# New durations for VectorE and ScalarE in the table that an order of instructions is planned with

## The chip, the cores and the metric

The kernel runs on one core of a Trainium2 chip. The metric is the device time of one execution in microseconds; three runs of the kernel before gave 955.95 to 956.46 us, with a median of 956.35 us. The engines are TensorE (PE in the profile, its weight loads PEld), VectorE (DVE), ScalarE (ACT), GpSimd (POOL) and SyncE (SP), which here issues DMAs. Every engine works through its own instructions strictly in the order in which the program lists them, and an instruction that waits for another engine holds up all that stand behind it on its own.

## The reference

Three layers follow each other, all in float32:

```python
# 1. attention, 8 batches x 8 heads, 576 positions of 64, causal by blocks of 64 positions
scores = q @ k.T / sqrt(64);  scores = where(block_i >= block_j, scores, -1e9)
attn = exp(scores - max); attn /= attn.sum() + 1e-9; x = attn @ v        # then 4608 tokens x 512
# 2. a feed-forward layer, 512 -> 2048 -> 512
h = x @ w_in
g = where(h > 0, h, exp(min(h, 0)) - 1);  y = g @ w_out
# 3. a soft mixture of 8 experts with 4 slots each
logits = y @ phi                                                          # 4608 x 32
d = softmax over tokens;  c = softmax over slots
slot_out = relu((d.T @ y) @ w1[e]) @ w2[e];  out = c @ slot_out
```

## The kernel before

The work has a prologue, a long middle part and a tail. In the prologue the weights are brought in and split: each word of `w_in` is rescaled, shifted and put together by bit operations (L424 or L426, L428, L431), and split into a high and a low float32r part (L441, L442). Beside it the first pairs of heads go through the attention. In the middle part 36 tiles of 128 tokens go through the second layer, 22 units of planning time apart, while TensorE works ahead on the attention of later pairs of heads. The tail computes the experts and writes the result.

One tile has four ranges of 512 columns of the second layer. A range is 12 matmuls in 4 blocks of three (`hm`, L808 to L810: high times high, high times low, low times high), with weights from `w0` to `w3`, one for each range. ScalarE then takes the exponential (L813), VectorE takes the minimum and subtracts 1 (L815), then takes the maximum with the matmul's result in PSUM (L818), and transposes (L826). Two PSUM banks take turns: range `r` uses bank `r % 2`, so the first matmul of a range waits until L818 of the range two before it has read the bank. A tile's routing follows: logits (L853), a copy (L876), sums (L880, L881), maxima (L885 to L894), two exponentials, a transpose on TensorE (L360 with `base` alone, "the turn"), a copy of its result (L904), and the weighted sum of slots (L919 on TensorE, L924 on VectorE).

The attention of a pair of heads has four groups of score matmuls (L568 to L576), each followed by fills with the mask (L584), row maxima (L587), exponentials (L590), sums and reciprocals (L602, L603), a scaling on GpSimd (L607), transposes by TensorE (L360 with `base` and `att`) or VectorE (L689) and the product with the values (L739 or L767).

None of this order is written out. Each operation is added to a plan with its engine or engines, a duration, what it reads and writes, and a priority (`key`). `Plan.order` (L126) is a list scheduler: it keeps a clock for each engine, starts an operation when the engine is free by the table's duration and its inputs have come by the table's durations plus a delay for each pair of engines (`HOPS`, L60: 0.13 to 0.23), and takes the ready one with the lowest key. Where an operation may run on two engines (copies on ScalarE or VectorE by `CP2`, the rescaling on ScalarE or GpSimd), the one that is free first takes it. Where TensorE would stand idle in two stretches of the program, the planner puts in small matmuls that compute nothing needed (L1200, `plan.fill`). The sequence that comes out is issued as it is; on the chip the engines wait for each other's semaphores, not for the planner's clock.

So a duration in the table costs no time itself. It moves instructions on all engines, picks the engine of some copies and sets the number of small matmuls.

Of the kernel before, what the change touches and what calls it, by code (L numbers as in the profile page):

```python
# [14 lines left out]
AF = mybir.ActivationFunctionType  # L15
# [3 lines left out]
P = 128  # L19
# [219 lines left out]
def attention_moe_kernel(ctx: ExitStack, tc, q, k, v, w_in, w_out, phi, w1, w2, consts, out):  # L239
# [103 lines left out]
    def cpdur(n, big=False):  # L343
        return (0.05 + n / 1200, 0.065 + n / 960)

# [203 lines left out]
    def wide(x):  # L549
        return S if x == "b" else P * (x[0] + 1)  # L550

    def pair_scores(n, fill, key):
# [32 lines left out]
        for x in units:  # L585
            c = nm_col + 9 * s + UNITS[x][0]
            add("DVE", 0.08 + wide(x) / 960, lambda e, x=x, c=c: nc.vector.tensor_reduce(  # L587
                out=f(c, 1), in_=pb(at(x), wide(x)), axis=AX.X, op=ALU.max, negate=True),
                r=keys(x), w=[("nm", s, x)], key=key)
            add("ACT", 0.50 + wide(x) / 1300, lambda e, x=x, c=c: nc.scalar.activation(  # L590
                f(pat(x, n), wide(x)), pb(at(x), wide(x)), AF.Exp, bias=f(c, 1), scale=1.0,
                accum_out=f(sum_col + 9 * s + UNITS[x][0], 1)),
                r=keys(x) + [("nm", s, x)], w=[pkey(x, n), ("sum", s, fill // 2)], key=key)

    def pair_weights(n, half, key):
# [8 lines left out]
        add("DVE", 0.35, rec, r=[("sum", s, half)], w=[("rs", s, half)], key=key)  # L604
        for x in units:
# [71 lines left out]
    def pair_swap(n, half, key):  # L677
# [5 lines left out]
        for x in HALVES[half]:  # L683
            if x == "b" or x[0] == 0:
                continue
            cs = min(x[0] + 1, 3)
            at, _, step = spots(x[0], x[1], 0)
            o = f(px, 4 * XW).rearrange("p (m b j) -> p b m j", m=4, j=32)[:, at:at + step * (cs - 1) + 1:step]
            add("DVE", 0.12 + P * cs / 960, lambda e, x=x, o=o, cs=cs: nc.vector.transpose(  # L689
                out=o, in_=f(pat(x, n), P * cs).rearrange("p (c m i) -> p c m i", c=cs, m=4)),  # L690
                r=[pkey(x, n)], w=[("px", sl, x)], key=key)
        both = f(py, 2 * YW).rearrange("p (h w) -> p h w", h=2)
        groups = ([("b", c) for c in range(4)], [((3, 0), 3), ((3, 1), 3), ("b", 4)]) if half == 0 else ([((0, 0), 0), ((0, 1), 0)],)
        for gi, blocks in enumerate(groups):
# [8 lines left out]
            def evac(e, g=g, tb=tb):  # L703
# [7 lines left out]
                else:  # L711
                    copy(e, both[:, :, 0:P], pb(tb, 256).rearrange("p (h x) -> p h x", h=2))
            add(*evict(n, (560, 430, 256)[g]), evac, r=[tk], w=[("py", sl, g)], key=key)
        if half == 0:
# [71 lines left out]
    def tile_split(i, key):  # L786
        s = i % 2
        r0 = (P * i) % RING
        halves = sorted({(P * i // S) % 2, ((P * i + P - 1) // S) % 2})
        xr_keys = [("xr", p, hf, j) for p in range(4) for hf in halves for j in range(2)]  # L790
        xv = f(XR, 4 * RING).rearrange("p (c t) -> p c t", t=RING)[:, :, r0:r0 + P]
        xh, xl = XH + 512 * s, XL + 512 * s
        add("ACT", 0.52, lambda e: nc.scalar.copy(fr(xh, 512).rearrange("p (c t) -> p c t", t=P), xv),  # L793
            r=xr_keys, w=[("xh", s)], key=key)
        add("POOL", 1.35, lambda e: nc.gpsimd.tensor_tensor(  # L795
            out=fr(xl, 512).rearrange("p (c t) -> p c t", t=P), in0=xv,
            in1=f(xh, 512).rearrange("p (c t) -> p c t", t=P), op=ALU.subtract),
            r=xr_keys + [("xh", s)], w=[("xl", s)], key=key)

    def tile_range(i, r, hb, gs, ts, kr):  # L800
# [4 lines left out]
        for kk in range(4):  # L805
# [62 lines left out]
    def tile_dispatch(tiles, gs, banks, lps, dtx, dx, kp, later=False):  # L868
# [6 lines left out]
        for t in range(n):  # L875
            add("DVE", 0.2, lambda e, t=t: nc.vector.tensor_copy(f(lps[t][0], P), pb(banks[t][0], P)),  # L876
                r=[banks[t][1]], w=[lps[t][1]], key=kp)
# [6 lines left out]
        ko, kn = "nmx%d" % ((i + 1) % 2), "nmx%d" % (i % 2)  # L884
        add("DVE", 0.07 + n * P / 960, lambda e: nc.vector.tensor_reduce(out=f(MXT, 1), in_=pb(reps, n * P), axis=AX.X, op=ALU.max, negate=True),  # L885
            r=[bk], w=["mxt"], key=kp)
        add("DVE", 0.1, lambda e: nc.vector.tensor_tensor(out=f(nmn, 1), in0=f(nmo, 1), in1=f(MXT, 1), op=ALU.min),
            r=[ko, "mxt"], w=[kn], key=kp)
        add("ACT", 0.3 + n * 0.1, lambda e: nc.scalar.activation(f(dtx[0], n * P), pb(reps, n * P), AF.Exp, bias=f(nmn, 1), accum_out=f(TSUM, 1)),
            r=[bk, kn], w=[dtx[1], "tsum"], key=kp)  # L890
        add("ACT", 0.22, lambda e: nc.scalar.activation(f(ALPHA, 1), f(nmo, 1), AF.Exp, bias=f(nmn, 1), scale=-1.0),
            r=[ko, kn], w=["alpha"], key=kp + 0.1)
        for t in range(n):
            add("DVE", 0.1, lambda e, t=t: nc.vector.tensor_reduce(out=f(NMC + t, 1), in_=pb(tok + NS * t, NS), axis=AX.X, op=ALU.max, negate=True),  # L894
                r=[bk], w=[("nmc", t)], key=kp + 0.2)
            add("ACT", 0.4, lambda e, t=t: nc.scalar.activation(f(C + NS * (i + t), NS), pb(tok + NS * t, NS), AF.Exp, bias=f(NMC + t, 1),
                                                                accum_out=f(CS + i + t, 1)),
                r=[bk, ("nmc", t)], w=["c", "cs"], key=kp + 0.2)
# [5 lines left out]
        add("DVE", 0.1, lambda e: nc.vector.tensor_copy(f(dx[0], n * NS).rearrange("p (t s) -> p t s", t=n),  # L904
                                                        pb(flip, n * P).rearrange("p (t x) -> p t x", t=n)[:, :, 0:NS]),
            r=[fk], w=[dx[1]], key=kp)
        add("DVE", 0.1, lambda e: nc.vector.scalar_tensor_tensor(
            out=f(SSUM, 1), in0=f(SSUM, 1), scalar=f(ALPHA, 1), in1=f(TSUM, 1), op0=ALU.mult, op1=ALU.add),
# [326 lines left out]
```

## Time and profile before

| | us |
|---|---|
| median of 3 runs | 956.35 |
| the profiled execution | 955.77 |
| its span from the first to the last instruction | 954.0 |
| TensorE busy | 908.7 (95%) |
| VectorE busy | 675.9 (71%) |
| ScalarE busy | 439.4 (46%) |
| GpSimd busy | 272.6 (29%) |

"Busy" is the time in which at least one instruction of the engine is under way; instructions of one engine overlap at their ends, so the sum of their durations is larger. A matmul's record also runs on past the start of the next one. Idle time is put down to what the next instruction waited for.

### The profile page before, as it was taken

The page shows a single profiled execution, that of the slowest core. Times are in us where ns is not written, and L with a number is a line of the kernel's source. Part 1 is how long each engine was busy: PE and PEld are TensorE (multiplying, and loading weights), DVE is VectorE, ACT ScalarE, POOL GpSimd, SP SyncE. Part 2 cuts the span into 40 slices and gives each one's busy share as a digit, 9 for nine tenths or more (in the row PEclk, how much of TensorE's full clock was granted, in tenths as well). Part 3 has the DMA queues.
Part 4 walks back from the last instruction along what each step waited for, and adds up shares of the span by engine and source line. Part 5 has one row for each costly group of instructions (what it writes and reads, how often), then busy time and mean ns, then how long its engine had stood idle before and what let it go on. Part 6 is the DMA issues. An engine that isn't in the chain of part 4 may idle for free.

```text
span 954.0 us, 19403 instructions
## 1 busy us (share of the span) xinstructions
PE 908.7 (95%) x6708; PEld 623.3 (65%) x6708; DVE 675.9 (71%) x1718; ACT 439.4 (46%) x1285; POOL 272.6 (29%) x428
## 2 busy tenths in 40 slices
PE   8889999999999999999999999999999999999992
PEld 6556777666666766676766666766776776766350
DVE  5887795668787887777888878887887844333160
ACT  5775655445445535444445445444444333322143
POOL 2863442133342332222323432332332210000000
PEclk9999999999999999999999999999999999999996
DMA  9846755647777785767677777667756498068969
GB/s 235 243 130 171 220 184 159 146 115 207 202 203 218 197 209 184 212 181 211 194 203 206 199 208 201 202 188 203 206 163 217 144 305 340 3 216 298 377 223 342
DMA packets 253217, 197.08 MB, mean 207 GB/s; under 512 B 183232, under 2 KB 206400, under 8 KB 250048
## 3 DMA queue, kind: packets, MB, share of 16 engines
q1 hardware_dynamic: 251920, 195.55, 69.1%
q8 instruction: 54, 0.88, 0.4%
q10 hardware_dynamic: 1200, 0.30, 0.1%
q14 instruction: 43, 0.35, 0.1%
HBM read 125.52 MB, written 70.25 MB: 205 GB/s over the span
## 4 chain that ended last, share of the span: by engine, by line
PE 74%; DVE 8%; DMA 7%; SPq 4%; ACT 2%; issue 2%; POOL 1%; ACTq 0%; DVEq 0%; POOLq 0%
PE ps L808 13%; PE ps L810 11%; PE ps L809 11%; PE ps L360 8%; PE ps L576 7%; PE ps L739 7%; SPq L355 4%; PE ps L919 3%; PE ps L568 2%; PE ps L853 2%; DMA att<-swapped 2%; DMA swapped<-att 2%; PE ps L767 2%; DVE base L587 2%; PE ps L460 1%
## 5 line engine op out<-in xcount | busy, mean ns | idle before, releaser
L808 PE MATMUL ps<-w,xhl 128*128 128x512 f32 x576 | 249.8, 434 | 7.8 <-DVE g L818 5.5
L607 POOL TENSOR_SCALAR att<-att,base 128x128 f32<-128x128 f32 (+4 forms) x288 | 181.0, 647 | 222.2 <-DVE base L603 151.0
L810 PE MATMUL ps<-w,xhl 128*128 128x512 f32 x576 | 226.8, 394 | 0.0
L809 PE MATMUL ps<-w,xhl 128*128 128x512 f32 x576 | 225.7, 392 | 0.0
L590 ACT ACTIVATE att<-ps,base 128x128 f32<-128x128 f32 (+4 forms) x288 | 157.4, 552 | 122.9 <-DVE base L587 121.0
L587 DVE TENSOR_REDUCE base<-ps 128x1 f32<-128x128 f32 (+4 forms) x288 | 135.7, 503 | 21.3 <-PE ps L572 12.2
L808 PEld LDWEIGHTS ps<-w,xhl 128*128 128x128 f32 x576 | 108.8, 189 | 52.0 <-issue 19.1
L813 ACT ACTIVATE xe<-ps 128x512 f32<-128x512 f32 x144 | 86.0, 600 | 115.0 <-PE ps L810 113.7
L810 PEld LDWEIGHTS ps<-w,xhl 128*128 128x128 f32 x576 | 108.1, 188 | 24.9
L336 ACT COPY att<-ps 128x128 f32<-128x128 f32 (+3 forms) x192 | 75.7, 434 | 95.8 <-PE ps L360 90.6
L809 PEld LDWEIGHTS ps<-w,xhl 128*128 128x128 f32 x576 | 108.9, 189 | 14.8
L815 DVE TENSOR_SCALAR xe<-xe 128x512 f32<-128x512 f32 x144 | 68.1, 473 | 67.0 <-ACT xe L813 65.6
L576 PE MATMUL ps<-att 64*128 64x128 f32 (+3 forms) x512 | 96.1, 468 | 1.0 <-ACT att L590 1.0
L360 PE MATMUL ps<-base,att 128*128 128x128 f32 (+1 forms) x496 | 83.2, 282 | 9.7 <-POOL att L607 8.5
L360 PEld LDWEIGHTS ps<-base,att 128*128 128x128 f32 (+1 forms) x496 | 58.0, 143 | 44.5 <-POOL att L607 17.6
L795 POOL TENSOR_TENSOR xhl<-xe,xhl 128x512 fp32r<-128x512 f32 x36 | 46.3, 1291 | 133.1 <-ACT xhl L793 127.0
L818 DVE TENSOR_TENSOR g<-xe,ps 128x512 f32<-128x512 f32 x108 | 73.3, 680 | 2.4
L689 DVE STREAM_TRANSPOSE att<-att 128x384 f32<-128x384 f32 x144 | 70.4, 507 | 5.3 <-POOL att L607 4.2
L739 PE MATMUL ps<-att 128*64 128x64 f32 (+4 forms) x864 | 71.9, 318 | 1.2 <-DMA att<-swapped 0.7
L576 PEld LDWEIGHTS ps<-att 64*128 64x128 f32 x512 | 42.0, 185 | 40.6 <-issue 14.1
L739 PEld LDWEIGHTS ps<-att 128*64 128x64 f32 x864 | 46.8, 137 | 32.3 <-issue 23.6
L826 DVE STREAM_TRANSPOSE g<-g 128x512 f32<-128x512 f32 x84 | 58.0, 695 | 1.7 <-DMA turned<-g 0.2
(134 smaller groups left out, 1115.1 us busy)
## 6 DMA issues: line engine op xcount, KB each, us to landing
turned<-g SPq DMA_DIRECT2D x60, 512.0 KB, 3.1
swapped<-att SPq DMA_DIRECT2D x24, 1024.0 KB, 4.6
g<-turned SPq DMA_DIRECT2D x120, 96.0 KB, 2.6
att<-in_moe_w_dram SPq DMA_DIRECT2D x11, 1024.0 KB, 11.8
att<-swapped SPq DMA_DIRECT2D x48, 192.0 KB, 3.9
att<-in_v_dram SPq DMA_DIRECT2D x64, 128.0 KB, 3.2
g<-in_moe_w_in_dram SPq DMA_DIRECT2D x16, 512.0 KB, 5.3
w_late<-in_moe_w_dram SPq DMA_DIRECT2D x8, 1024.0 KB, 6.9
```

What stands on the lines that cost most here:

```text
L336: nc.scalar.copy(o, i)
L360: mm(o, lhsT=i, rhs=f(IDN + base, n, base, base + n), start=True, stop=True, is_transpose=True)
L576: mm(pb(at((u, h)), P * (u + 1)), lhsT=f(qt + P * u, P, 64 * h, 64 * h + 64), rhs=f(kt, P * (u + 1), 64 * h, 64 * h + 64), start=True, sto ...
L587: add("DVE", 0.08 + wide(x) / 960, lambda e, x=x, c=c: nc.vector.tensor_reduce(out=f(c, 1), in_=pb(at(x), wide(x)), axis=AX.X, op=ALU.max, ...
L590: add("ACT", 0.50 + wide(x) / 1300, lambda e, x=x, c=c: nc.scalar.activation(f(pat(x, n), wide(x)), pb(at(x), wide(x)), AF.Exp, bias=f(c, ...
L607: add("POOL", (0.28 + wide(x) / 1050) * (1.3 if n < 8 else 1.0), lambda e, x=x, p=p: nc.gpsimd.tensor_scalar(out=f(p, wide(x)), in0=f(p, w ...
L739: mm(pb(o, w, 64 * h, 64 * h + 64), lhsT=f(vs + 320 * h + D * c, D), rhs=rhs(h), start=start, stop=stop)
L808: mm(pb(bank, 512), lhsT=fr(xh + P * kk, P), rhs=hi, start=(kk == 0), stop=False)
L809: mm(pb(bank, 512), lhsT=fr(xh + P * kk, P), rhs=lo, start=False, stop=False)
L810: mm(pb(bank, 512), lhsT=fr(xl + P * kk, P), rhs=hi, start=False, stop=(kk == 3))
L813: add("ACT", 0.48, lambda e: nc.scalar.activation(f(ee, 512), pb(bank, 512), AF.Exp), r=[("h", hb)], w=[("e", hb)], key=kr)
L818: add("DVE", 0.6, lambda e: nc.vector.tensor_tensor(out=f(g, 512), in0=f(ee, 512), in1=pb(bank, 512), op=ALU.max), r=[("e", hb), ("h", hb) ...
```

## The change

Nineteen lines of the kernel's plan get other durations for VectorE and ScalarE; no operation, buffer, priority or dependency is touched. The core of it:

```diff
     def cpdur(n, big=False):
-        return (0.05 + n / 1200, 0.065 + n / 960)
+        return (0.165 + n / 1200, 0.15 + n / 960)
...
-            add("DVE", 0.08 + wide(x) / 960, lambda e, x=x, c=c: nc.vector.tensor_reduce(
+            add("DVE", 0.14 + wide(x) / 960, lambda e, x=x, c=c: nc.vector.tensor_reduce(
...
-        add("ACT", 0.48, lambda e: nc.scalar.activation(f(ee, 512), pb(bank, 512), AF.Exp),
+        add("ACT", 0.6, lambda e: nc.scalar.activation(f(ee, 512), pb(bank, 512), AF.Exp),
...
-        add("DVE", 0.335, lambda e: nc.vector.tensor_scalar(
+        add("DVE", 0.47, lambda e: nc.vector.tensor_scalar(
...
-        add("DVE", 0.6, lambda e: nc.vector.tensor_tensor(
+        add("DVE", 0.68, lambda e: nc.vector.tensor_tensor(
```

`cpdur` gives a copy's duration on ScalarE and on VectorE. The others shown are L587, L813, L815 and L818. The rest is of the same kind: L602 with L603 (0.35 to 0.38), L689 (0.12 to 0.15 plus a part by size), the copies behind the transposes (L713), L793 (0.52 to 0.62), and the small operations of the routing (0.1 to 0.4 become 0.17 to 0.57). The durations for TensorE, GpSimd and the DMAs and the delays in `HOPS` stay.

In numbers of instructions: TensorE has 504 small matmuls (L1200) instead of 456. VectorE has 70 copies from PSUM (L338) instead of 56 and ScalarE has 12 instructions fewer. Two rescalings move from GpSimd to ScalarE. The 576 blocks of three matmuls stand in 247 uninterrupted runs instead of 236.

The order is changed nearly everywhere. Three places follow. The first is on VectorE where range 3 of tile 3 ends (its L818 frees the bank for range 1 of tile 4). Before, with `base` the area of the routing's small results, `xe` the exponentials and `g` the layer's result:

```order
L907 SCALAR_TENSOR_TENSOR base<-base 128x1
L904 COPY base<-ps 128x32
L924 SCALAR_TENSOR_TENSOR base<-base,ps 128x512
L815 TENSOR_SCALAR xe<-xe 128x512
L584 MEMSET ps 64x64 x2
L818 TENSOR_TENSOR g<-xe,ps 128x512
```

The same L815 and L818 after the change:

```order
L815 TENSOR_SCALAR xe<-xe 128x512
L876 COPY base<-ps 128x128
L587 TENSOR_REDUCE base<-ps 128x1 x4
L818 TENSOR_TENSOR g<-xe,ps 128x512
L689 STREAM_TRANSPOSE att<-att 128x3x4x32 x2
L885 TENSOR_REDUCE base<-ps 128x1
```

L904 and L924, which need the turn and the weighted sum from TensorE, stood ahead of L815 and L818 and now stand behind them.

The second place is on TensorE at tile 10, where range 2 (weights `w2`) begins behind range 1 (`w1`). Before, with `xhl` the tile's tokens and `att` the attention's area:

```order
L808 MATMUL ps_72<-w1_69,xhl_67 128x512
L809 MATMUL ps_72<-w1_69,xhl_67 128x512
L810 MATMUL ps_72<-w1_69,xhl_67 128x512
L360 MATMUL ps_72<-base_63 128x128
L808 MATMUL ps_72<-w1_69,xhl_67 128x512
L809 MATMUL ps_72<-w1_69,xhl_67 128x512
L810 MATMUL ps_72<-w1_69,xhl_67 128x512
L808 MATMUL ps_72<-w2_70,xhl_67 128x512
```

After:

```order
L739 MATMUL ps_72<-att_66 64x64 x2
L739 MATMUL ps_72<-att_66 64x256 x2
L739 MATMUL ps_72<-att_66 64x64 x2
L739 MATMUL ps_72<-att_66 64x192 x2
L739 MATMUL ps_72<-att_66 64x64 x2
L360 MATMUL ps_72<-base_63 128x128
L576 MATMUL ps_72<-att_66 128x384 x2
L576 MATMUL ps_72<-att_66 128x128 x2
L808 MATMUL ps_72<-w1_69,xhl_67 128x512
L809 MATMUL ps_72<-w1_69,xhl_67 128x512
L810 MATMUL ps_72<-w1_69,xhl_67 128x512
L808 MATMUL ps_72<-w2_70,xhl_67 128x512
```

A product with the values and a group of scores now stand inside range 1, so more of TensorE's work lies between the end of range 0 and the start of range 2, which use the same bank.

The third place is on VectorE where range 3 of tile 26 ends. Before:

```order
L587 TENSOR_REDUCE base<-ps 128x1
L815 TENSOR_SCALAR xe<-xe 128x512
L904 COPY base<-ps 128x32
L818 TENSOR_TENSOR att<-xe,ps 128x512
L826 STREAM_TRANSPOSE g<-att 128x4x4x32
```

After:

```order
L815 TENSOR_SCALAR xe<-xe 128x512
L689 STREAM_TRANSPOSE att<-att 128x3x4x32
L904 COPY base<-ps 128x32
L689 STREAM_TRANSPOSE att<-att 128x3x4x32
L587 TENSOR_REDUCE base<-ps 128x1 x4
L818 TENSOR_TENSOR att<-xe,ps 128x512
```

Here a transpose and four row maxima come between L904, which needs the turn, and L818.

## Rows read from the trace of the kernel before

**Rows 1.** The page: busy time by engine, granted TensorE clock in 40 slices.
```profile
PE 908.7 (95%) x6708; PEld 623.3 (65%) x6708; DVE 675.9 (71%) x1718; ACT 439.4 (46%) x1285; POOL 272.6 (29%) x428
...
PEclk9999999999999999999999999999999999999996
```

**Rows 2.** Stretches: length; busy of PE, PEld, DVE, ACT, POOL; clock; DMA.
```profile
16.00:54.00 38.00, 30.39 (x277) 21.36 (x277) 35.23 (x90) 28.96 (x84) 29.29 (x32) 1.00 0.86 223
54.00:58.00 4.00, 4.00 (x19) 1.85 (x17) 1.95 (x5) 1.96 (x6) 1.78 (x2) 0.59 0.52 140
58.00:86.00 28.00, 26.21 (x262) 18.83 (x259) 24.45 (x55) 19.24 (x50) 17.33 (x19) 1.00 0.34 97
86.00:190.00 104.00, 103.34 (x715) 74.62 (x714) 75.44 (x182) 57.82 (x160) 31.15 (x43) 1.00 0.67 189
190.00:768.00 578.00, 568.96 (x4067) 395.18 (x4066) 467.63 (x1238) 267.60 (x851) 184.47 (x318) 1.00 0.69 195
```

**Rows 3.** Waits of PE, 86 to 866 us: total, times, longest.
```profile
PE ps L808 <- DVE g L818: 5.5, 6, 2.0
PE ps L808 <- DVE att L818: 2.2, 3, 1.0
```

**Rows 4.** Timeline of DVE, 205 to 216 us: start, length, instructions, idle before.
```profile
210.25 0.19 DVE L904 COPY base<-ps 128x32 f32<-128x32 f32 x1 [1.01 <-PE ps L360]
211.98 0.75 DVE L924 SCALAR_TENSOR_TENSOR base<-base,ps 128x512 f32<-128x512 f32 x1 [1.54 <-PE ps L919]
212.64 1.04 DVE L815 TENSOR_SCALAR xe<-xe 128x512 f32<-128x512 f32 x1
...
213.79 0.66 DVE L818 TENSOR_TENSOR g<-xe,ps 128x512 f32<-128x512 f32 x1
214.38 0.73 DVE L587 TENSOR_REDUCE base<-ps 128x1 f32<-128x256 f32 x2
```

**Rows 5.** Timeline of PE, the same stretch.
```profile
211.84 0.70 PE L576 MATMUL ps<-att 64*128 64x256 f32 x4
214.51 0.50 PE L808 MATMUL ps<-w,xhl 128*128 128x512 f32 x1 [1.97 <-DVE g L818]
214.84 0.39 PE L809 MATMUL ps<-w,xhl 128*128 128x512 f32 x1
215.07 0.40 PE L810 MATMUL ps<-w,xhl 128*128 128x512 f32 x1
215.31 0.40 PE L808 MATMUL ps<-w,xhl 128*128 128x512 f32 x1
```

**Rows 6.** Groups by line and form: count, busy, mean ns, idle before.
```profile
L808 PE MATMUL ps<-w,xhl 128*128 128x512 f32 x576 | 249.8, 434 | 7.8 <-DVE g L818 5.5 <-DVE att L818 2.2
L809 PE MATMUL ps<-w,xhl 128*128 128x512 f32 x576 | 225.7, 392 | 0.0
...
L813 ACT ACTIVATE xe<-ps 128x512 f32<-128x512 f32 x144 | 86.0, 600 | 115.0 <-PE ps L810 113.7
L818 DVE TENSOR_TENSOR g<-xe,ps 128x512 f32<-128x512 f32 x108 | 73.3, 680 | 2.4
L815 DVE TENSOR_SCALAR xe<-xe 128x512 f32<-128x512 f32 x144 | 68.1, 473 | 67.0 <-ACT xe L813 65.6
...
L689 DVE STREAM_TRANSPOSE att<-att 128x384 f32<-128x384 f32 x96 | 51.4, 551 | 4.3 <-POOL att L607 3.4 <-DMA g<-turned 0.4 <-DMA att<-swapped 0.2
...
L1200 PE MATMUL ps<-base 128*128 128x128 bf16 x456 | 35.0, 226 | 1.5 <-DVE base L382 1.5
...
L587 DVE TENSOR_REDUCE base<-ps 128x1 f32<-128x384 f32 x64 | 32.8, 541 | 0.0
...
L338 DVE COPY g<-ps 128x512 f32<-128x512 f32 x8 | 5.5, 691 | 17.0 <-PE ps L360 16.2 <-DMA att<-wo_f 0.8
```

**Rows 7.** Timeline of ACT, 272 to 279 us.
```profile
272.93 0.60 ACT L813 ACTIVATE xe<-ps 128x512 f32<-128x512 f32 x1 [2.72 <-PE ps L810]
273.42 0.61 ACT L793 CAST xhl<-xe 128x512 fp32r<-128x512 f32 x1
```

**Rows 8.** Waits of PE in the first 86 us: total, times, longest.
```profile
PE ps L360 <- POOL att L607: 8.5, 10, 1.8
```

More of the change, by code (lines that the diff above doesn't have):

```diff
@@ L603, in rec @@
             nc.vector.reciprocal(f(rs, nc_), f(rs, nc_))
-        add("DVE", 0.35, rec, r=[("sum", s, half)], w=[("rs", s, half)], key=key)
+        add("DVE", 0.38, rec, r=[("sum", s, half)], w=[("rs", s, half)], key=key)
         for x in units:
@@ L688, in pair_swap @@
             o = f(px, 4 * XW).rearrange("p (m b j) -> p b m j", m=4, j=32)[:, at:at + step * (cs - 1) + 1:step]
-            add("DVE", 0.12 + P * cs / 960, lambda e, x=x, o=o, cs=cs: nc.vector.transpose(
+            add("DVE", 0.15 + P * cs / 960, lambda e, x=x, o=o, cs=cs: nc.vector.transpose(
                 out=o, in_=f(pat(x, n), P * cs).rearrange("p (c m i) -> p c m i", c=cs, m=4)),
@@ L712, in evac @@
                     copy(e, both[:, :, 0:P], pb(tb, 256).rearrange("p (h x) -> p h x", h=2))
-            add(*evict(n, (560, 430, 256)[g]), evac, r=[tk], w=[("py", sl, g)], key=key)
+            add(*(evict(n, (512, 384, 256)[g])[0], tuple(x + (0.16 if g < 2 else 0.0) for x in cpdur((512, 384, 256)[g]))), evac, r=[tk], w=[("py", sl, g)], key=key)
         if half == 0:
@@ L884, in tile_dispatch @@
         ko, kn = "nmx%d" % ((i + 1) % 2), "nmx%d" % (i % 2)
-        add("DVE", 0.07 + n * P / 960, lambda e: nc.vector.tensor_reduce(out=f(MXT, 1), in_=pb(reps, n * P), axis=AX.X, op=ALU.max, negate=True),
+        add("DVE", 0.14 + n * P / 960, lambda e: nc.vector.tensor_reduce(out=f(MXT, 1), in_=pb(reps, n * P), axis=AX.X, op=ALU.max, negate=True),
             r=[bk], w=["mxt"], key=kp)
-        add("DVE", 0.1, lambda e: nc.vector.tensor_tensor(out=f(nmn, 1), in0=f(nmo, 1), in1=f(MXT, 1), op=ALU.min),
+        add("DVE", 0.17, lambda e: nc.vector.tensor_tensor(out=f(nmn, 1), in0=f(nmo, 1), in1=f(MXT, 1), op=ALU.min),
             r=[ko, "mxt"], w=[kn], key=kp)
-        add("ACT", 0.3 + n * 0.1, lambda e: nc.scalar.activation(f(dtx[0], n * P), pb(reps, n * P), AF.Exp, bias=f(nmn, 1), accum_out=f(TSUM, 1)),
+        add("ACT", 0.47 + n * 0.1, lambda e: nc.scalar.activation(f(dtx[0], n * P), pb(reps, n * P), AF.Exp, bias=f(nmn, 1), accum_out=f(TSUM, 1)),
             r=[bk, kn], w=[dtx[1], "tsum"], key=kp)
-        add("ACT", 0.22, lambda e: nc.scalar.activation(f(ALPHA, 1), f(nmo, 1), AF.Exp, bias=f(nmn, 1), scale=-1.0),
+        add("ACT", 0.29, lambda e: nc.scalar.activation(f(ALPHA, 1), f(nmo, 1), AF.Exp, bias=f(nmn, 1), scale=-1.0),
             r=[ko, kn], w=["alpha"], key=kp + 0.1)
         for t in range(n):
-            add("DVE", 0.1, lambda e, t=t: nc.vector.tensor_reduce(out=f(NMC + t, 1), in_=pb(tok + NS * t, NS), axis=AX.X, op=ALU.max, negate=True),
+            add("DVE", 0.18, lambda e, t=t: nc.vector.tensor_reduce(out=f(NMC + t, 1), in_=pb(tok + NS * t, NS), axis=AX.X, op=ALU.max, negate=True),
                 r=[bk], w=[("nmc", t)], key=kp + 0.2)
-            add("ACT", 0.4, lambda e, t=t: nc.scalar.activation(f(C + NS * (i + t), NS), pb(tok + NS * t, NS), AF.Exp, bias=f(NMC + t, 1),
+            add("ACT", 0.49, lambda e, t=t: nc.scalar.activation(f(C + NS * (i + t), NS), pb(tok + NS * t, NS), AF.Exp, bias=f(NMC + t, 1),
                                                                 accum_out=f(CS + i + t, 1)),
```

10 lines of the change are left out of this document (5 added, 5 removed).

## The prediction

> **What bounds the kernel now.** I read the page first, then the stretches, then TensorE's waits, then the timeline around the longest of them. The page has TensorE busy for 908.7 of 954.0 us [rows 1], so the question is where the other 45 us lie and which of them an order can touch. The stretches answer it [rows 2]: from 86 to 190 us TensorE is busy for 103.34 of 104 us, from 190 to 768 us for 568.96 of 578, while before 86 us it is busy 30.39 of 38 us and 26.21 of 28, with VectorE at 35.23 of 38 there. So the prologue hangs on VectorE and the chain of waits around it, and everything behind it on TensorE. In the long middle part the reader is to see one kind of wait: the first matmul of a range, L808, waits for L818, which has to read its bank: 9 times, 5.5 + 2.2 = 7.7 us [rows 3]. A matmul's record runs 0.39 us while the next one starts 0.23 us behind it [rows 5], so each wait hides some 0.16 us more; 9 times that is 1.4, and the loss is about 9.2 us. The longest shows how it comes about [rows 4, 5]. L904 and L924 are small things of the routing that wait for TensorE (1.01 and 1.54 us idle). L815 and L818, which TensorE needs, stand behind them. VectorE stood still with work in hand, and then TensorE stood still for 1.97 us. It isn't VectorE's load but the order in its queue, against TensorE's progress.
>
> **The change, part by part.** It alters no instruction's cost, so every term is one of order.
>
> Waits for L818. At the place of the longest wait the new order has L815 and L818 ahead of L904 and L924; at the second place shown, TensorE has a product with the values and a group of scores more between the two ranges that share a bank. I went through the nine places with a wait. In each, either VectorE's queue has been cleared in this way or TensorE has more to do in between, so I take all 9.2 us out: -9.2. What is late next there? The other inputs of a range (weights, tokens) are old by then, so TensorE simply goes on. The third place shown speaks the other way: L904 waits for the turn, and behind it now stand a transpose (551 ns) and four row maxima, two of them of 541 ns [rows 6], before L818, while TensorE comes to the range soon after the turn. I find three places of this kind in the new order. Their price isn't in the trace; the nearest rows are the waits of the same kind, 7.7 / 9 = 0.86 us on the mean and 2.0 at most [rows 3], with the hidden 0.16 some 1.0 to 2.2 us; from nothing (if TensorE is late anyway) to 2.2 each. I take 1.1, nearer the mean: +3.3, bounds 0 to +6.6.
>
> Runs of matmuls. The three matmuls of a block are float32r, most else on TensorE is not, and the first L808 behind something else shows 0.50 us where one in the middle of a run shows 0.40, and the next starts 0.33 behind it instead of 0.23 [rows 5]. The mean tells the same: (434 - 392) x 576 = 24 us [rows 6], over 236 runs 0.10 us each. The new order has 247 runs: 11 x 0.10 = +1.1. As TensorE is the bound there, nothing hides it.
>
> Small matmuls. 48 more L1200 at 35.0 / 456 = 0.077 us [rows 6] are 3.7 us of TensorE. They stand in the prologue, where TensorE is idle for 7.6 us between 16 and 54 us and 1.8 between 58 and 86 [rows 2], and waits 8.5 us for GpSimd's scaling [rows 8]; I cost them at nothing, and at +3.7 if they were all to stand ahead of something that is already waiting. [...]
>
> The prologue's queues. Three of the 16 copies behind the weights' transposes go from ScalarE to VectorE, which is the fuller (35.23 of 38 us against 28.96 [rows 2]): 3 x 0.691 us [rows 6] = 2.1 if all of it lies on the path. Two rescalings leave GpSimd, which sits in the same chain. On each engine I count nearly the same work ahead of what the first range waits for. I take 0 for the prologue, and -3 to +4 as bounds, the sums of what stands here. What moves in SP's queue are loads in the prologue by a place or two; the last stretch, the writing of the result, is as before in kind, and I cost both at nothing, with the prologue's bounds as cover.
>
> Copies moved in the middle. VectorE gets 14 copies from PSUM more, at most 14 x 0.691 = 9.7 us, over a stretch in which it is idle for 578 - 467.63 = 110 us [rows 2]. Hidden, unless they come between L813 and L818 of a range, and then they are one more wait of the kind priced above.
>
> The sum: -9.2 + 3.3 + 1.1 + 0 = -4.8 us on the profiled execution, 955.77 to 950.97. That execution lies 0.58 us under the median of the runs, so for the median 956.35 - 4.8 = 951.5 us.
>
> **Is the new table right?** That an order could be better for it isn't given, since the old table was not simply wrong. L793 starts 0.49 us behind L813, whose record is 0.60 [rows 7]; the table had 0.48 and has 0.60 now. L587 starts 0.59 us behind L818, whose record in that place is 0.66 [rows 4]; the table had 0.60, now 0.68. So the old numbers are nearly the distance from start to start, the new ones are the records, and the planner adds its delay of 0.13 to 0.2 us per hop to either. It now thinks a range's chain L813, L815, L818 longer by 0.12 + 0.135 + 0.08 = 0.34 us and VectorE fuller than it is. I still forecast a gain, because a planner that believes VectorE late gives TensorE something else to do in between, and at run time early results cost nothing; the places shown are of this sort.
>
> [...]
>
> **The rivals.**
>
> 1. The overstated table spoils VectorE's queue: slower. The planner puts fillers (L689, L587, L904) between L815 and L818 because it believes that there is time, and TensorE's ranges then wait. Its place is the third one shown. For it: L904 behind the turn, with 551 + 2 x 541 ns and more behind it; the planner's queue for VectorE is now fuller than the real one, so what it puts in a gap that isn't there would pile up. Against it: what VectorE does faster than planned comes early, and gaps between ranges on TensorE grew at the old places. It decides from about seven such places on (9.2 - 1.1 = 8.1 us, at 1.1 each). With twelve, 12 x 1.1 + 1.1 - 9.2 = +5.1, so 961.5 us.
>
> 2. The waits only change places: no difference. With seven new ones, 7 x 1.1 + 1.1 - 9.2 = -0.4, so 956 us. For it: three of them are easy to find, and VectorE is still a queue in order at 81% (467.63 / 578). Against it: four more would have to be as long as the mean.
>
> [...]
>
> **Chances and range.** The forecast 0.43, rival 1 0.24, rival 2 0.20, rival 3 0.13. What a measurement of this kernel can tell from no change is 0.2%, 1.9 us. The forecast and rival 3 are faster by more: 0.56. Rival 2 is the same, 0.20, and rival 1 slower, 0.24. The forecast's own range is 947.5 to 955.5 us: the bounds on the new waits (-3.3, +3.3) with a part of the prologue's. The range for 8 in 10 goes from 946 us, the far side of rival 3, to 961 us, the middle of rival 1.
>
> **What would show it right or wrong.** In the profile after, TensorE's waits for L818 should sum to 2 to 4 us instead of 7.7, in other places; the long one near 212 us should be gone, with L904 behind L818 in VectorE's timeline. L808's mean should be a little up by the runs, and down by the waits hidden in it. TensorE should be busy for 570 of 578 us or more in the middle. The first range should start within 3 us of where it did (86 us), and the clock before it may stay up. I am wrong if the waits for L818 sum to 7 us or more, which is rival 2 or 1, or if the first range starts later by more than 4 us.

## The result and the profile after

The kernel after took 968.58 us (median of 4 runs, 967.84 to 974.41), the kernel before beside it 956.15 us. The ratio is 1.0149, with a 95% interval of 1.0106 to 1.0192: slower by about 12 us, where 951.5 us had been forecast. The profiled execution took 968.02 us, 12.25 more than that of before.

The page of after, for [rows 1]:

```profile
PE 914.7 (95%) x6756; PEld 630.9 (65%) x6756; DVE 682.8 (71%) x1732; ACT 437.7 (45%) x1273; POOL 269.6 (28%) x426
...
PEclk9999999999999999999999999999999999999996
```

The stretches of after, for [rows 2] (length; busy of PE, PEld, DVE, ACT, POOL; clock; DMA):

```profile
58.00:86.00 28.00, 21.71 (x205) 14.64 (x203) 21.33 (x47) 15.75 (x43) 18.96 (x17) 0.94 0.29 87
86.00:190.00 104.00, 102.56 (x740) 75.51 (x738) 76.22 (x180) 59.50 (x156) 29.81 (x41) 1.00 0.68 186
190.00:768.00 578.00, 563.30 (x3994) 391.16 (x3993) 463.47 (x1229) 263.19 (x834) 180.59 (x312) 1.00 0.68 192
```

Between 190 and 768 us TensorE is now idle for 14.7 us instead of 9.0. Fixed times cut the two kernels at different work, though. So here are the same two views cut at the first and the last L808, the start and the end of the second layer. Before:

```profile
0.00:85.70 85.70, 73.25 (x674) 52.03 (x674) 66.56 (x160) 56.65 (x152) 50.28 (x63) 0.98 0.69 184
85.70:865.20 779.50, 768.27 (x5459) 537.93 (x5459) 583.18 (x1507) 355.55 (x1078) 222.34 (x366) 1.00 0.68 197
```

After:

```profile
0.00:89.60 89.60, 77.55 (x717) 56.02 (x717) 68.71 (x161) 57.06 (x152) 51.78 (x64) 0.94 0.70 190
89.60:877.90 788.30, 770.38 (x5462) 541.64 (x5459) 587.12 (x1519) 353.76 (x1067) 217.84 (x363) 1.00 0.66 193
```

The prologue is 3.9 us longer and the layer 8.8; what follows it is 0.5 shorter (955.77 - 865.2 against 968.02 - 877.9). That is the whole 12.2 us. In the layer 6.7 of the 8.8 us are idle time of TensorE (17.92 against 11.23) and 2.1 are busy time. In the prologue it is the other way round: the idle time stays (12.05 against 12.45 us), and TensorE is busy 4.3 us longer, with 43 more instructions (42 of them small matmuls, 362 instead of 320) and a granted clock of 0.94 instead of 0.98.

TensorE's waits from 86 to 866 us in the kernel after (total, times, longest), for [rows 3]:

```profile
PE ps L808 <- DVE g L818: 6.3, 7, 1.7
PE ps L739 <- DMA g<-turned: 2.9, 1, 2.9
PE ps L576 <- ACT att L590: 2.2, 1, 2.2
PE ps L360 <- ACT att L336: 1.8, 3, 0.8
PE ps L808 <- DVE att L818: 1.5, 2, 1.1
PE ps L739 <- DMA att<-swapped: 0.9, 1, 0.9
```

The waits for L818 sum to 7.8 us as before (7.7), again nine of them, eight at other places. The three kinds behind them (2.9, 2.2 and 1.8 us) are new in size: in the same stretch of before no kind of wait but L808's has more than 0.9 us. Near 212 us VectorE's queue is cleared as the prediction had it [rows 4, 5]: L818 now stands ahead of L904 and L924 (start, length, instructions, idle before):

```profile
208.46 1.01 DVE L587 TENSOR_REDUCE base<-ps 128x1 f32<-128x384 f32 x2
...
210.21 0.68 DVE L818 TENSOR_TENSOR g<-xe,ps 128x512 f32<-128x512 f32 x1
...
214.02 0.15 DVE L904 COPY base<-ps 128x32 f32<-128x32 f32 x1
...
215.47 0.75 DVE L924 SCALAR_TENSOR_TENSOR base<-base,ps 128x512 f32<-128x512 f32 x1
```

What came in elsewhere is seen on VectorE at 715 us:

```profile
714.94 0.38 DVE L584 MEMSET ps<- 64x64 f32 x4 [1.38 <-PE ps L576]
715.23 0.48 DVE L815 TENSOR_SCALAR xe<-xe 128x512 f32<-128x512 f32 x1
715.64 0.56 DVE L689 STREAM_TRANSPOSE att<-att 128x384 f32<-128x384 f32 x1
716.13 0.14 DVE L904 COPY base<-ps 128x32 f32<-128x32 f32 x1
716.20 0.55 DVE L689 STREAM_TRANSPOSE att<-att 128x384 f32<-128x384 f32 x1
716.68 1.37 DVE L587 TENSOR_REDUCE base<-ps 128x1 f32<-128x384 f32 x4
717.99 0.66 DVE L818 TENSOR_TENSOR att<-xe,ps 128x512 f32<-128x512 f32 x1
```

and on TensorE:

```profile
717.13 0.52 PE L360 MATMUL ps<-base,att 128*128 128x128 f32 x3
718.70 0.50 PE L808 MATMUL ps<-w,xhl 128*128 128x512 f32 x1 [1.05 <-DVE att L818]
```

This is the third place of the prediction in full: VectorE stands idle for 1.38 us ahead of fills with the mask, which wait for the scores of L576; then two transposes and four row maxima go between L815 and L818, and a range waits for L818.

Behind one wait more time is lost than its own length. On TensorE, at 400 us:

```profile
400.22 0.39 PE L810 MATMUL ps<-w,xhl 128*128 128x512 f32 x1
402.84 1.04 PE L576 MATMUL ps<-att 64*128 64x256 f32 x4 [2.23 <-ACT att L590]
403.81 2.74 PE L739 MATMUL ps<-att 128*64 128x128 f32 x16
```

and in the chain of waits (start, us, what), first a product with the values as it usually is:

```profile
379.00 2.88 PE ps L739 x36
...
403.88 4.54 PE ps L739 x36
```

Behind the wait of 2.23 us the granted clock is 0.63 on the mean from 403.4 to 407.9 us (1.00 up to 404 us, 0.50 from 405 us on), and the same 36 matmuls take 1.66 us longer. The longest wait of the layer, 2.94 us ahead of an L739 at 600.57 us, is not followed by a lower clock (1.00). Both stretches (as in [rows 2]):

```profile
403.40:407.90 4.50, 4.50 (x33) 2.50 (x33) 3.38 (x10) 1.18 (x5) 2.24 (x6) 0.63 0.50 142
600.60:605.00 4.40, 3.92 (x40) 2.59 (x40) 3.52 (x10) 3.02 (x12) 1.10 (x1) 1.00 0.38 123
```

The 11 more runs show in L808's mean, 437 ns instead of 434, with L809's at 392 in both [rows 6]: 3 ns x 576 = 1.7 us, where 1.1 had been costed.

```profile
L808 PE MATMUL ps<-w,xhl 128*128 128x512 f32 x576 | 251.8, 437 | 7.8 <-DVE g L818 6.3 <-DVE att L818 1.5
```

The two together are more than the 2.1 us of added busy time.

### The profile page after: what moved, and what is told of

Same layout as the page of the kernel before. It is cut to its first block, busy times and chain, and to the rows that moved or that the text cites. A ratio compares the mean times of both kernels' runs of the same rounds, so it can differ in the third digit from the quotient of the medians.

```text
span 966.2 us, 19503 instructions
## 1 busy us (share of the span) xinstructions
PE 914.7 (95%) x6756; PEld 630.9 (65%) x6756; DVE 682.8 (71%) x1732; ACT 437.7 (45%) x1273; POOL 269.6 (28%) x426
## 4 chain that ended last, share of the span: by engine, by line
PE 80%; DVE 6%; DMA 6%; POOL 2%; issue 2%; ACT 1%; SPq 1%; ACTq 0%; DVEq 0%; POOLq 0%
PE ps L808 14%; PE ps L810 12%; PE ps L809 12%; PE ps L360 8%; PE ps L576 8%; PE ps L739 7%; PE ps L919 3%; PE ps L853 3%; PE ps L568 2%; PE ps L1200 2%; POOL att L607 2%; DMA g<-turned 1%; PE ps L767 1%; DVE base L587 1%; DMA att<-in_moe_w_dram 1%
## 5 line engine op out<-in xcount | busy, mean ns | idle before, releaser
L808 PE MATMUL ps<-w,xhl 128*128 128x512 f32 x576 | 251.8, 437 | 7.8 <-DVE g L818 6.3
L607 POOL TENSOR_SCALAR att<-att,base 128x128 f32<-128x128 f32 (+4 forms) x288 | 178.0, 635 | 270.0 <-DVE base L603 215.8
L809 PE MATMUL ps<-w,xhl 128*128 128x512 f32 x576 | 226.0, 392 | 0.0
L587 DVE TENSOR_REDUCE base<-ps 128x1 f32<-128x128 f32 (+4 forms) x288 | 135.5, 501 | 24.3 <-PE ps L572 12.4
L808 PEld LDWEIGHTS ps<-w,xhl 128*128 128x128 f32 x576 | 108.6, 188 | 61.1 <-issue 22.2
L813 ACT ACTIVATE xe<-ps 128x512 f32<-128x512 f32 x144 | 86.2, 599 | 130.5 <-PE ps L810 128.9
L809 PEld LDWEIGHTS ps<-w,xhl 128*128 128x128 f32 x576 | 109.0, 189 | 14.7
L336 ACT COPY att<-ps 128x512 f32<-128x512 f32 (+3 forms) x184 | 73.1, 433 | 87.6 <-PE ps L360 83.6
L815 DVE TENSOR_SCALAR xe<-xe 128x512 f32<-128x512 f32 x144 | 67.6, 469 | 57.7 <-ACT xe L813 57.4
L576 PE MATMUL ps<-att 64*128 64x128 f32 (+3 forms) x512 | 96.7, 469 | 3.3 <-ACT att L590 3.3
L795 POOL TENSOR_TENSOR xhl<-xe,xhl 128x512 fp32r<-128x512 f32 x36 | 47.5, 1323 | 161.6 <-ACT xhl L793 161.4
L360 PEld LDWEIGHTS ps<-base,att 128*128 128x128 f32 (+1 forms) x496 | 58.9, 145 | 46.5 <-POOL att L607 14.8
L739 PE MATMUL ps<-att 128*64 128x64 f32 (+4 forms) x864 | 73.1, 323 | 3.8 <-DMA g<-turned 2.9
L689 DVE STREAM_TRANSPOSE att<-att 128x384 f32<-128x384 f32 x144 | 70.5, 511 | 5.9 <-POOL att L607 5.0
L818 DVE TENSOR_TENSOR g<-xe,ps 128x512 f32<-128x512 f32 x108 | 73.0, 676 | 2.0
L739 PEld LDWEIGHTS ps<-att 128*64 128x64 f32 x864 | 47.2, 140 | 36.3 <-issue 23.2
L576 PEld LDWEIGHTS ps<-att 64*128 64x128 f32 x512 | 42.6, 185 | 39.8 <-issue 16.4
```

Source lines behind the costliest of these rows:

```text
L336: nc.scalar.copy(o, i)
L360: mm(o, lhsT=i, rhs=f(IDN + base, n, base, base + n), start=True, stop=True, is_transpose=True)
L576: mm(pb(at((u, h)), P * (u + 1)), lhsT=f(qt + P * u, P, 64 * h, 64 * h + 64), rhs=f(kt, P * (u + 1), 64 * h, 64 * h + 64), start=True, sto ...
L587: add("DVE", 0.14 + wide(x) / 960, lambda e, x=x, c=c: nc.vector.tensor_reduce(out=f(c, 1), in_=pb(at(x), wide(x)), axis=AX.X, op=ALU.max, ...
L607: add("POOL", (0.28 + wide(x) / 1050) * (1.3 if n < 8 else 1.0), lambda e, x=x, p=p: nc.gpsimd.tensor_scalar(out=f(p, wide(x)), in0=f(p, w ...
L739: mm(pb(o, w, 64 * h, 64 * h + 64), lhsT=f(vs + 320 * h + D * c, D), rhs=rhs(h), start=start, stop=stop)
```

## The experiments

The layer's length and TensorE's waits in it are told from the first to the last L808 of one profiled execution of each kernel; executions of one kernel differ by some us (e1's profiled one took 959.36 us, its median is 963.02). The ratio is to the executions of the kernel before that ran beside the run (medians of 955.89 to 957.31 us), not to the first row. The theories: A, the new numbers overstate what VectorE and ScalarE need, and the planner misplaces work; later split into A1 (they are *held* too long in the plan) and A2 (their results are *seen* too late). B, any other table is another draw, and the old order was a lucky one. C, ScalarE's numbers do it. D (B' in the expectations of m1 and m2), an order planned with a longer-held VectorE is worse for any VectorE.

| kernel | us, median | ratio to before, 95% interval | first L808 | layer | TensorE's waits in it | of these L808 |
|---|---|---|---|---|---|---|
| before | 956.15 | | 85.7 | 779.5 | 11.1 | 7.7 |
| after | 968.58 | 1.0149 (1.0106 to 1.0192) | 89.6 | 788.3 | 17.7 | 7.8 |
| e1_prologue | 963.02 | 1.0069 (1.0046 to 1.0093) | 88.7 | 781.4 | 12.3 | 6.0 |
| e2_middle | 973.08 | 1.0158 (1.0121 to 1.0196) | 85.3 | 797.9 | 23.3 | 18.9 |
| e3_old_x101 | 956.25 | 0.9990 (0.9973 to 1.0007) | 84.9 | 781.9 | 11.9 | 9.2 |
| e4_new_x099 | 972.92 | 1.0170 (1.0137 to 1.0202) | 93.5 | 792.0 | 19.0 | 8.1 |
| f1_seen | 959.40 | 1.0023 (0.9999 to 1.0047) | 85.8 | 779.9 | 11.3 | 6.4 |
| f2_held | 973.18 | 1.0181 (1.0158 to 1.0203) | 86.7 | 795.6 | 23.4 | 19.9 |
| f3_new_pe112 | 974.83 | 1.0188 (1.0165 to 1.0211) | 92.3 | 790.0 | 19.8 | 2.7 |
| f4_old_x094 | 959.78 | 1.0038 (1.0024 to 1.0052) | 84.6 | 784.8 | 15.9 | 5.4 |
| h1_new_dve | 966.89 | 1.0100 (1.0070 to 1.0131) | 81.8 | 792.4 | 19.3 | 10.3 |
| h2_new_act | 959.92 | 1.0023 (1.0003 to 1.0044) | 89.0 | 779.6 | 11.0 | 7.2 |
| i1_old_first | 961.38 | 1.0033 (1.0009 to 1.0058) | 86.0 | 785.7 | 14.8 | 0.8 |
| i2_new_first | 973.60 | 1.0165 (1.0126 to 1.0203) | 87.8 | 792.8 | 19.5 | 4.0 |
| k1_dve_prologue | 960.23 | 1.0040 (1.0022 to 1.0058) | 83.1 | 787.6 | 18.9 | 10.9 |
| m1_old_slow | 963.19 | 1.0068 (1.0047 to 1.0089) | 86.0 | 788.1 | 16.8 | 11.0 |
| m2_new_slow | 975.83 | 1.0207 (1.0185 to 1.0228) | 87.7 | 803.6 | 24.7 | 10.5 |
| m3_old_slow32 | 970.18 | 1.0139 (1.0110 to 1.0168) | 86.3 | 793.1 | 20.0 | 13.7 |
| m4_new_slow32 | 982.31 | 1.0260 (1.0225 to 1.0295) | 90.5 | 801.4 | 22.7 | 10.8 |
| n_held_seen | 956.09 | 0.9991 (0.9975 to 1.0006) | 92.8 | 772.6 | 6.1 | 3.3 |

**Where, and is it luck.** The plan is made of events at times `t`, with `t` < 0 in the prologue. e1 and e2 take the new numbers on one side only; e3 and e4 scale one table a little.

```diff
+    for t, fn in ev:
+        new[0] = t < 0; fn()        # e1; e2: t >= 0
...
+        i, dur = len(self.ops), tuple(d * 1.01 if e in ("ACT", "DVE") else d for e, d in zip(engs, dur))   # e3; e4: new table, 0.99
```

> New durations only for what is added to the plan for times below 0 (the prologue's pairs of heads and weights), the old ones for the tiles, the later pairs and the tail. The changed kernel's profile lost 3.9 us up to the first range (its first matmul at 89.6 us instead of 85.7) and some 8 us behind it. Theory A, the new table misplaces work at each stage because it books the records' lengths and the delays on top of them: the prologue alone costs its own part, first range 3 to 5 us later, time 959 to 962 us. Theory B, any change of the table throws the order elsewhere and the order before was a fortunate one: the middle is reshuffled as well by the other start, so the time is anywhere from 956 to 968 us and the middle loses several us with its old durations.

> The other half: old durations for what is added for times below 0, the new ones for the tiles, the later pairs and the tail. Theory A: the prologue is as before (first range within 1 us of 85.7), the middle loses its 8 us, time 962 to 966 us. Theory B: the middle's loss is a matter of luck, 954 to 968 us. With both halves, A wants e1 and e2 to add up to the 12 us of the whole change.

> The old table with every duration of ScalarE and VectorE 1% longer: far nearer to the old table than the change is (it adds 12% to VectorE's sum and 14% to ScalarE's). The order it plans still differs in most places. Theory A: 1% of double counting costs next to nothing, 955 to 957.5 us. Theory B: a new draw from the same urn, 958 to 970 us, with the waits for L818 in other places and a sum of 5 to 12 us.

> The new table with every duration of ScalarE and VectorE 1% shorter. Theory A: as the changed kernel, 967 to 969.5 us. Theory B: another draw, 956 to 970 us, off the changed kernel's 968.6 by several us in either direction.

Each side costs. e1 starts the layer 3 us later and makes it 1.9 us longer; e2 starts it as before and makes it 18 us longer. The old order isn't one lucky table: 1% on it changes nothing, and 1% off the new one doesn't bring the time back. That spoke against B in its plain form. A missed too, though: e1, e2 and e4 came out slower than its ranges (e2 and e4 slower than B's as well), and the halves, which it wanted to add up to the whole, sum to 2.3% (0.7 + 1.6) where the whole change costs 1.5%.

**Held or seen.** f1 and f2 give the planner two durations for each operation, one for its engine and one for those who wait for its result. f3 lengthens TensorE in the plan as the other two engines were; f4 goes the other way.

```diff
-                fin = now + d
+                fin = now + getattr(d, "seen", d)
...
-        add("DVE", 0.6, lambda e: nc.vector.tensor_tensor(
+        add("DVE", Two(0.6, 0.68), lambda e: nc.vector.tensor_tensor(      # f1: held old, seen new; f2: (0.68, 0.6)
...
+        i, dur = len(self.ops), tuple(d * 1.12 if e in ("PE",) else d ...)  # f3, new table; f4: ACT, DVE * 0.94, old table
```

> The order is planned with the old durations for how long VectorE and ScalarE are held, and with the new ones for when the result is there for whoever waits for it. Theory A1 (the new table hurts because it makes VectorE and ScalarE fuller than they are: its records overlap, and the planner lays them end to end): about as before, 954 to 960 us. Theory A2 (it hurts because the result comes later in the plan than on the chip, so that TensorE is given other work at the wrong places): about as after, 965 to 973. Theory B (any other table is only another draw): anywhere between 953 and 973, without relation to the other halves.

> The other half: VectorE and ScalarE are held for the new durations, and who waits for a result is planned with the old ones. Theory A1: about as after, 965 to 973 us, with TensorE's waits for L818 at 7 us or more. Theory A2: about as before, 954 to 960. Theory B: anywhere between, and f1 and f2 may both be slow or both be as before.

> The new table as it is, and TensorE's durations in the plan 12% longer, as those of VectorE and ScalarE have grown (the plan's VectorE goes from 665 to 745 us with the new table, TensorE's stays at 837 where the chip takes some 894 from start to start). Theory A1, in the form that only the balance between the engines counts: most of the loss goes, 955 to 961 us. Theory A2: the hops count as before, so a part of the loss goes at most, 962 to 970. Theory B: anywhere between 953 and 973.

> The old table with VectorE's and ScalarE's durations 6% shorter. Theories A1 and A2 (the old table is about right, and what counts is how far the plan's engines are from the chip's): little changes, 953 to 960 us, since it is half as far from the old table as the new one and on the other side. Theory B: anywhere between 953 and 973, as likely slow as not.

In the layer it is the held time. f1's layer is as long as before's, f2's 16 us longer. TensorE's waits of f1 in the layer:

```profile
PE ps L808 <- DVE att L818: 3.7, 4, 1.8
PE ps L808 <- DVE g L818: 2.7, 5, 0.9
```

and of f2:

```profile
PE ps L808 <- DVE g L818: 12.3, 10, 2.8
PE ps L808 <- DVE att L818: 7.6, 4, 2.9
```

f3 came out as no theory had it, with a first range 6.6 us and a layer 10.5 us behind before's. Its waits for L818 are down to 2.7 us, and most of the layer's waiting is for DMAs (the plan now takes them for relatively quick; that this is why isn't shown):

```profile
PE ps L739 <- DMA att<-swapped: 6.3, 4, 3.2
PE ps L739 <- DMA g<-turned: 5.1, 5, 1.7
```

f4 is slower by 0.4%: shorter isn't better either.

**Which engine.** h1 takes the new numbers for VectorE alone, h2 for ScalarE alone.

```diff
-        return (0.05 + n / 1200, 0.065 + n / 960)
+        return (0.05 + n / 1200, 0.15 + n / 960)      # h1, and every add("DVE", ...); h2: (0.165 ..., 0.065 ...)
```

> The new durations for VectorE alone, ScalarE's as before. Theory A1 (held times that are too long spoil the order in VectorE's queue, the fuller of the two): the middle part is lost as in the kernel after, VectorE stands idle at a blocked head with an L815 ready behind it for 12 us or more (6.7 us in the kernel before, 12.7 after), and the time is 964 to 973 us. Theory C (ScalarE's new durations do it, by the waits of L576 for L590 and by the copies that move off ScalarE): 954 to 960 us.

> The new durations for ScalarE alone. Theory A1: the middle part is as before (idle at a blocked head with an L815 ready behind it 5 to 8 us), and what is lost lies in the prologue, where ScalarE has 16 copies: 955 to 961 us. Theory C: 964 to 973 us.

The two losses come apart. VectorE's numbers make the layer 13 us longer and the prologue 3.9 shorter; ScalarE's leave the layer alone and make the prologue 3.3 longer. C is out for the layer and fits the prologue. The idle time that both expectations name (VectorE at a head that waits, an L815 ready behind it), counted with every idle stretch of the layer, is 7.5 us in before, 16.1 in after, 12.9 in h1 and 12.3 in h2. A1 had 5 to 8 for h2. So this idle time is nearly as long in h2 as in h1, and h2's layer lost nothing by it.

**Is a wait worth its length?** i1 takes the waits for L818 away from the old order without touching a duration, i2 does it to the new one.

```diff
-            w=[("e", hb)], key=kr)
+            w=[("e", hb)], key=kr - 22)               # L815, and L818 in the same way
```

> The old table; L815 and L818 get a key that is lower by two ranges, so that VectorE takes them first whenever both they and something else are ready in the plan. Theory A1 with the step of the prediction that waits for L818 cost their length: the waits for L818 fall from 7.7 us to 4 or less and the time by 2 to 5 us, 951 to 954 us, as long as nothing else waits for what is put back. If what is put back (row maxima, transposes) is waited for instead: 956 to 960 us, with waits of L576 or L739 in their place.

> The new table with the same lower key for L815 and L818. If the whole loss were that others stand ahead of L815 and L818 in VectorE's queue: as i1 or as before, 952 to 960 us. Theory A1, by which the held times that are too long put every kind of work in the wrong place: the waits for L818 get fewer, waits of other kinds stay, 962 to 970 us.

In i1 the waits for L818 fell by 6.9 us, from 7.7 to 0.8, and the kernel became slower, by 0.33% (0.09 to 0.58). TensorE's waits of i1 in the layer:

```profile
PE ps L739 <- DMA att<-swapped: 3.2, 3, 1.4
PE ps L360 <- POOL xhl L795: 2.4, 3, 0.9
PE ps L576 <- ACT att L590: 2.2, 3, 1.8
PE ps L460 <- ACT base L336: 1.8, 2, 1.1
PE ps L360 <- ACT base L889: 1.1, 1, 1.1
PE ps L360 <- DVE base L924: 0.9, 1, 0.9
PE ps L808 <- DVE g L818: 0.8, 1, 0.8
```

Others are waited for instead, with interest: 14.8 us in all for 11.1. Among them are L576 and L739, as expected, but also GpSimd's L795; that each is late because of what was put back isn't shown, and at 961.38 us the kernel lies over both expected ranges. In i2 the waits for L818 fell from 7.8 us to 4.0 and the others grew from 9.9 to 15.5. Its 973.60 us is above A1's range of 962 to 970; that the whole loss were L815 and L818 standing too far back in VectorE's queue is out.

**Does the new order fit a slower VectorE?** A1 says that an order suits the held times that it was planned with. m1 to m4 leave each order as it is and put a small write behind every VectorE operation, of one column (m1, m2) or 32 (m3, m4).

```diff
-            fn(e)
+            fn(e), e == "DVE" and nc.vector.memset(f(JUNK, 1), 0.0)
```

> The old table and its order, but VectorE is really held longer: behind each of its operations stands a small write of one column that nobody waits for (about the length by which the new table holds VectorE longer on the mean). It is to be compared with m2, the same with the new table. Theory A1 (an order fits the held times that it was planned with): this one loses what the kernel after loses, 966 to 985 us, with waits of TensorE for L818 of 12 us or more. Theory B' (the new order is worse whatever the engines do): it loses as much as m2 loses against after, and stays 1% or more under m2.

> The new table and its order with the same small writes on VectorE. Theory A1: the new order loses little by them, as it reckons with such a VectorE: 968 to 978 us, the same as m1 within 0.3% or faster. Theory B': 12 us or more over m1.

> As m1 (old table and order), but the small write behind each operation of VectorE has 32 columns instead of one. In m1 the distances from start to start grew by 0.01 to 0.05 us, some 33 us in all, where the new table holds VectorE 80 us longer; with 32 columns it should be about 90. Theory A1 (an order fits the held times that it was planned with): at this size the old order is the wrong one, 975 to 990 us, and no faster than m4. Theory D (the plan with the longer held times is the worse order, also on a VectorE that has them): 968 to 978 us, and still 8 us or more under m4.

> As m2 (new table and order), with 32 columns. Theory A1: 975 to 985 us, no slower than m3. Theory D: 980 to 990 us, 8 us or more over m3.

The new order is 12.6 us behind the old one with one column and 12.1 with 32, as it is without (12.4). VectorE's busy time is 714.0 us in m1 and 736.0 in m3, 38 and 60 more than before; the 60 are three quarters of the 80 us by which the new table lengthens the plan's VectorE. The write is the same behind every operation, where the table adds 0.03 to 0.2 us by kind; a VectorE that is slower kind by kind as in the table was not run. A1 would have had the gap close as VectorE slows; it doesn't at all, and D came out in both numbers of m3 and m4 (m2 lies where A1 had it, but m1 is as far ahead as before). The writes do lengthen the waits: the profile puts them down to the small write (L1207) that stands behind L818. In m3, then in m4:

```profile
PE ps L808 <- DVE base L1207: 13.7, 15, 2.4
```

```profile
PE ps L808 <- DVE base L1207: 10.8, 10, 2.6
PE ps L739 <- DMA att<-swapped: 3.3, 2, 2.9
PE ps L576 <- ACT att L590: 3.0, 2, 2.8
```

The new order does wait less for VectorE here, as A1 has it, but its other waits (12 us of 22.7) stay.

**A version that beats both?** k1 keeps h1's gain in the prologue and the old table behind it. n_held_seen holds VectorE and ScalarE, for ten kinds of operation, for the distance from start to start in the trace of before, and leaves the times at which results are seen.

```diff
+        new[0] = t < 0; fn()                          # k1, for add("DVE", ...) alone
...
+            add("DVE", Two(0.063 + wide(x) / 960, 0.08 + wide(x) / 960), ...     # n_held_seen, L587 and nine more
+            add("ACT", Two(0.236 + wide(x) / 1200, 0.50 + wide(x) / 1300), ...   # L590
```

> The new durations of VectorE for what is planned ahead of the first token tile, the old ones behind it and for ScalarE throughout. With VectorE's new durations alone (h1) the first range started at 81.8 us instead of 85.7, and with ScalarE's alone (h2) at 89.0. Theory A1 for the middle part, and the prologue gaining from VectorE's: 951 to 954 us, a version that beats both. Theory B for the prologue (its start is another draw, and what is gained there is lost behind it): 956 to 960 us.

> The old table, with the held times of ten kinds of operation set to the distance from start to start in the trace of the kernel before (L587 0.063 us plus columns / 960, L590 0.236 plus columns / 1200, L689 0.06 plus columns / 960, L815 0.398, L826 0.608 and so on), and the times at which results are seen left as they were. If an order is the better the nearer the held times are to the chip's: 950 to 954 us, a version that beats both. If the old numbers were near enough, and what is left is the luck of one order among many: 954 to 961 us.

Neither. k1 starts the layer 2.6 us earlier and then has one of 787.6 us, 8.1 longer than before's, with the same durations in it (this execution took 962.1 us, 1.9 over k1's median): what stands ahead changes the order behind, as B had it. n_held_seen has the shortest layer of all kernels:

```profile
0.00:92.80 92.80, 78.40 (x695) 55.51 (x695) 69.86 (x168) 60.80 (x160) 48.82 (x59) 0.94 0.72 193
92.80:865.40 772.60, 766.34 (x5449) 535.52 (x5447) 583.90 (x1504) 354.51 (x1070) 218.50 (x364) 1.00 0.68 196
```

Its layer gains 6.9 us and its prologue loses 7.1. Those held times behind the prologue alone, with the old table in it, were not run.

## Why the prediction was wrong

**The step that failed** is the first term of the sum: "I take all 9.2 us out". Eight of the nine old waits did go (the shortest, 0.2 us at tile 23, grew to 0.4), and eight others came: the sum is 7.8 us, where the prediction had three new ones with 3.3. That is rival 2's account, and by the prediction's own condition (7 us or more) its forecast fell there; TensorE is busy for 563.3 of the 578 us, where 570 or more were to show it right. (7.7 + 1.4 is 9.1, not 9.2; that changes nothing.) Reading the old places in the new order shows what becomes of them, and says nothing of the places that one hasn't picked.

**The term that was missing** is larger. The sum had waits for L818 only. The layer's waits of other kinds went from 3.4 us (11.1 - 7.7) to 9.9 (17.7 - 7.8), and behind one of them the clock was lower (0.63 on the mean from 403.4 to 407.9 us). i1 shows that this is no accident of the one table: without any change of durations, 6.9 us of waits for L818 taken out gave back nothing. TensorE, busy for 98.6% of the layer before, waited here for several engines and queues by turns, and a wait removed from one of them was not time gained.

**The prologue, costed at nothing with -3 to +4 as bounds**, came out at +3.9. I hid 48 small matmuls in TensorE's idle time; the idle time is as long as before, and busy time was added. The low ends (-3 here, and the 946 us on the far side of rival 3) take in a gain by way of the clock from small matmuls ahead of the first range, a term that no run shows: with 42 more of them the clock was lower instead (0.94 for 0.98). The order alone doesn't set it, though. Up to the first range i2 has the order of after on TensorE, VectorE, ScalarE and GpSimd, instruction by instruction, and its profiled execution had a clock of 0.98 and started the layer at 87.8 us:

```profile
0.00:87.80 87.80, 75.64 (x716) 54.93 (x717) 67.99 (x161) 56.72 (x152) 50.23 (x64) 0.98 0.71 193
```

So with one order the start differs by 1.8 us from execution to execution. At the clock of before it is 2.1 us later in i2 and 3.0 in e1 (the same order but for the last few matmuls). (h1 and k1 are one order up to there as well, with 81.8 and 83.1 us.) The later start comes with ScalarE's numbers (h2: 3.3 us at a clock of 0.98), yet f1 and f2, with both engines' new numbers as seen or as held times alone, start 0.1 and 1.0 us later, and n_held_seen starts 7.1 later with shorter held times. What in the prologue's chain moved isn't settled.

**What held**: the 11 more runs (1.7 us for 1.1), the tail, the copies moved in the middle (no wait of TensorE in the layer is for one of L338), the place at 212 us cleared.

**Rival 1 had the right sign, at too small a chance, and its reason holds in part.** "Is the new table right?" found that the new numbers are records and the old ones distances from start to start, and the rest of the trace bears it out: where nothing is idle between them, the instruction behind L587 over 384 columns starts 0.46 us after it (two take 1.01 us in the line at 208.46 us above), where L587's record is 0.541 [rows 6], the old table had 0.48 and the new has 0.54. Beside 384 / 960 = 0.40 us for the columns, as the table has it, the record has 0.14 us more, the distance 0.06. I argued that a planner which thinks VectorE late only gives TensorE more to do in between. f2 and h1 show the opposite for the held part. Rival 1's path, more waits for L818, is seen in f2 (19.9 us), e2 (18.9) and h1 (10.3), but not in the kernel after (7.8). And its reason, a table that doesn't match the chip, isn't the whole of it: by m3 and m4 the order stays worse on a VectorE that is held longer.

**What stays open** is why a longer-held VectorE gives a worse order for either. Seven kernels plan the layer with such a VectorE (after, e2, e4, f2, f3, h1, i2): 788.3 to 797.9 us. Nine don't, or by 1% (before, e1, e3, f1, f4, h2, i1, k1, n_held_seen): 772.6 to 787.6. (m1 to m4 have another VectorE and stand aside.) The two sets don't overlap, though by 0.7 us in one execution of each, which is less than executions of one kernel differ by; the ratios in the table, of several executions each, lie apart as well (1.0100 to 1.0188 against 0.9990 to 1.0069, where only the intervals of h1 and e1 overlap). Within each set the order still makes 10 and 15 us. At 715 us one sees a queue in which VectorE first waits and then takes transposes and row maxima ahead of L818; that this is how it comes about everywhere is argued, not shown, and h2, with nearly as much of such idle time as h1 and no loss in the layer, speaks against it as the whole account.

## What to carry to other kernels

A change of a planner's table is a new order, and is costed by its total idle time on the bound engine, not by what becomes of the old waits: give the waits that can't be seen yet a term of their own, about as large as those removed. Set the time for which an engine is held from the distance between starts, not from the length of records, and keep it apart from when its result is seen: records as held times cost 1.8% here (f2), as seen times 0.2% (f1). Measured distances brought nothing over the old table's numbers (n_held_seen). Measure a few neighbours of a table (here 1% and 6% off, and one stage at a time) before a difference of 1% is put down to its numbers.

## What the runs showed of the hardware

After a wait of 2.23 us on TensorE in the kernel after, the granted clock was 0.63 on the mean from 403.4 to 407.9 us, and the same 36 matmuls took 4.54 us instead of 2.88; behind the wait of 1.97 us in the kernel before [rows 5], and behind one of 2.94 us in the kernel after, the clock stayed at 1.00. So the length of a wait alone doesn't tell what the clock did here. Nor does the order: the prologue of after and i2, one order, ran at 0.94 and 0.98. A write of 32 columns behind each of 1643 VectorE operations (m3), 85 ns each by its record and 139.7 us in all, added only 60 us to VectorE's busy time and 14 us to the kernel: on the mean 37 ns of a write's 85 came on top of VectorE's busy time.
